# Another order of the steps of a two-part kernel: x transposes and halo copies earlier in SyncE's queue, head and tail sums of a chunk side by side

## The chip, the cores and the metric

The kernel runs on one core of a Trainium2 chip. The metric is the device time of one execution in microseconds (us), the median over runs. The engines are named as the profile names them: PE (TensorE matmuls; PEld its weight loads), DVE (VectorE), ACT (ScalarE), POOL (GpSimd) and SP (SyncE, which here only issues DMAs). A "q" behind an engine (SPq, POOLq) means its queue of instructions.

## The reference

Two independent layers are computed on inputs of 2048 positions x 448 channels, and their outputs stand side by side in one array of 2048 x 896 (bfloat16).

```python
# part A: a linear state space layer with complex, diagonal state
Lam_bar = exp(dt * Lam);  B_bar = ((Lam_bar - 1) / Lam)[:, None] * Bmat
Bu = einsum("bld,pd->blp", x, B_bar)
h[t] = Lam_bar * h[t-1] + Bu[t]                       # t = 0 .. 2047
y = 2 * einsum("blp,dp->bld", h, Cmat).real + x * Dskip
# part B: attention of 16 heads (28 wide) to 8 positions: t, t-2, ..., t-14
q, k, v = split(x @ wqkv)
logits[t, w] = q[t] . k[t - 2w] * 28 ** -0.5          # -1e9 where t - 2w < 0
o[t] = sum_w softmax(logits[t])[w] * v[t - 2w]
out = o @ wo
```

## The kernel before

Each part is cut into small methods, and one string, `ORDER` (L751), lists the calls: `plan` (L786) reads it word by word and calls the method, so the string sets the order of the instructions on PE, DVE, ACT and SP. Each of these engines executes its own instructions in that order and waits only for semaphores; so a step that waits holds everything behind it on its engine. POOL's order is left to a scheduler. A step's name is a letter and its arguments; a trailing A or V says whether ACT or DVE carries out a copy from PSUM. PSUM tiles come from three rings: "mm" (four buffers), "pt" (two) and "lg" (two). A PE step takes a buffer when one has been released by its copy, so a late copy can hold PE.

Part B works on four chunks c of 512 positions.

- `P.c.g.w`: projection of q (w = 0) or k (w = 1), group g of 128 channels, four matmuls (L191); g = 3 is the tail, the last 64 channels of q and k together. `p...` copies it out (L83 on ACT, L88 on DVE). Trailing arguments pick some of the four slices of the contraction.
- `R.c.s` (DVE, L239): products of q with four shifted windows of k; `T.c` (L244): the same for the tail. `S.c.s` (PE, L254) and `St.c.s` (L261) sum them over each head with 32-column matmuls, s = 0, 1 being windows 0-3 and 4-7: the head sums and the tail sums. `St.0.1` adds the mask (L266).
- `s`, `mt`, `mr`, `mb`, `ms`, `me`: copy of the logits (L83), transposes (L276), max (DVE, L280), its copy (L83 or L88), its subtraction on PE (L290), exp (ACT, L296). `N`, `n`: back-transposes with sums (L305), reciprocal and product (DVE, L311, L312).
- `V.j`, `v.j`: v for positions 16p + j (L216, and a copy). `Z` (SP, L183) and `H` (L228, L229) are DMAs that write the halo, the 14 positions ahead of each partition's 16: `H.r0.r1` needs the v that it copies, `H.0.6` v.2 to v.7, `H.6.10` v.8 to v.11, `H.10.14` v.12 to v.15.
- `u.j.w` (DVE, L325): attention times v for positions j to j+3 and window w; `d` (DVE, L330) adds one of these to the sum; `f` (POOL, L334) adds one to another by an accumulating DMA. `tu.j` (SP, L338) transposes the result by DMA, and for the last four `tm`, `te` do it on PE, ACT and DVE (L347, L351, L352). `O`, `o`, `od`: the product with wo (L358), copy, output DMA (L373; L368 for the last two).

Part A has a state of 448 complex numbers, seven tiles m of 128. The 16 positions of a partition are handled as four a times four b.

- `X.a.b` (SP, L418 and L419): two DMA transposes that load x for positions 4a + b. `L.b.m` (PE, L600) multiplies them by the input matrix; it needs X.0.b to X.3.b. For odd b it adds the state of b - 1 (L603), for b = 3 also that of 1 (L605).
- `pp`, `pe`, `tb` (four pieces), `pg`, `M`, `B`, `b`: parameters, tables of sines and exponents, the matrices (L558 on DVE, 14 instructions L563 on ACT), the input matrix (L571, copy, and a memset on POOL, L577).
- `la`, `le`, `ro`, `sn`, `bk`, `be`: the last positions, and a scan over the partitions' blocks in two parts (0 and 1) that goes PE, DVE, PE, DVE, PE, ACT. `G`, `g`, `C`, `c`: corrections of the states. With V, one addition on DVE (L674, L693); with A, an identity matmul more on PE (L665, L683) and a copy on ACT (L676, L695).
- `sc` (SP, L582): four DMA transposes of the output matrix. `Y.a.b`, `y.a.b`: output (11 matmuls, L708, L711), copy to one of three buffers `ya`, output DMA on SP (L717).

SP issues, ahead of all steps, the loads of part B's x (L106, L108), weights and B matrices; then its DMAs stand in the order of the string.

Of the kernel before, what the change touches and what calls it, by code (L numbers as in the profile page):

```python
# [748 lines left out]


ORDER = """  # L751
    xa X.2.1 P.0.1.1.0.3 pp X.3.1 lw X.2.2 X.0.1 X.0.0 P.0.0.1.0.3 P.0.1.0.0.3 P.0.1.0.3.4 p.0.1.0.A P.0.2.1
    P.0.1.1.3.4 p.0.1.1.A P.0.0.1.3.4 p.0.0.1.A X.1.2 p.0.2.1.A P.0.0.0.0.3 P.0.0.0.3.4 P.0.2.0 p.0.0.0.A
    P.1.0.1 p.0.2.0.A pe tb R.0.1.1.2 P.1.2.0 p.1.2.0.A P.1.1.1 P.2.1.1 R.0.0.1.2 p.1.0.1.A p.2.1.1.A X.3.2
    P.0.3.0 p.0.3.0.A R.0.0.0.1 P.1.2.1 p.1.1.1.A p.1.2.1.A P.2.0.1 R.0.0.2.3 P.1.1.0 p.1.1.0.A P.1.0.0 S.0.0
    R.0.1.2.3 P.1.3.0 T.0 St.0.0 R.0.1.0.1 S.0.1 p.1.0.0.A p.2.0.1.A R.1.0 V.14 Z P.3.1.1 p.1.3.0.A tb p.3.1.1.A
    tb tb P.2.2.0 P.2.0.0 v.14.A R.1.1 X.3.0 P.2.1.0 p.2.1.0.A St.0.1 p.2.2.0.A P.3.0.1 p.3.0.1.A V.7 M.3.V
    v.7.A P.2.3.0 P.2.2.1 X.0.3 s.0.A T.1 mt.0 p.2.3.0.A P.3.2.1 p.3.2.1.A S.1.0 St.1.0 mr.0 p.2.2.1.A V.13 V.15
    S.1.1 St.1.1 p.2.0.0.A V.9 v.15.A P.3.2.0 pg B.3 mb.0.V R.2.0 ms.0 v.13.A v.9.A p.3.2.0.A V.2 me.0 V.8 v.8.A
    T.2 V.4 R.2.1 s.1.A B.0 b.3.A P.3.0.0 p.3.0.0.A P.3.1.0 p.3.1.0.A mt.1 mr.1 X.1.1 b.0.A S.2.0 P.3.3.0 mb.1.V  # L760
    p.3.3.0.A St.2.0 S.2.1 St.2.1 s.2.A V.1 v.1.A v.2.A v.4.A R.3.0 V.3 B.2 V.10 B.5 v.10.A ms.1 V.6 V.0 me.1
    V.11 T.3 v.3.A R.3.1 b.2.A mt.2 v.11.V mr.2 S.3.0 V.12 St.3.0 v.6.A b.5.A X.2.0 M.1.A S.3.1 St.3.1 B.1 X.0.2
    s.3.A L.2.0 mb.2.V pa M.4.V X.1.0 mt.3 H.6.10 V.5 ms.2 M.2.V mr.3 mb.3.V v.5.V L.2.2 v.12.A al l.2.0.A me.2
    ms.3 M.0.V sk H.10.14 L.0.0 b.1.A me.3 N.0 l.2.2.V N.3 n.3 n.0 L.0.3 u.0.3 u.0.4 lc v.0.A H.0.6 L.0.1
    l.0.1.A u.0.2 u.0.0 B.4 l.0.0.A L.1.1 L.2.3 f.0.2 u.0.5 B.6 l.0.3.A L.1.0 l.1.0.A u.0.1 u.0.6 f.0.4 u.0.7
    L.0.2 l.0.2.A N.12 d.0.1 N.6 L.2.1 l.1.1.A L.1.2 L.0.5 X.2.3 L.1.3 l.2.3.A n.12 n.6 d.0.2 u.4.3 l.2.1.A
    u.4.1 X.3.3 X.1.3 b.4.A l.1.3.A L.3.1 L.3.3 l.3.1.A L.0.4 d.0.4 l.0.5.A l.1.2.A L.3.2 l.3.2.A f.0.6 L.2.4
    N.15 b.6.A n.15 d.0.6 l.3.3.A L.3.0 l.0.4.A L.1.4 l.3.0.A L.2.5 L.0.6 N.9 sa la.0 l.2.5.A l.1.4.A L.1.5
    l.1.5.A L.3.5 l.3.5.A u.4.0 u.4.5 u.4.4 f.4.4 le.0 l.0.6.A tu.0 l.2.4.A sm u.4.2 f.4.2 ro.0 sn.0 L.2.6
    l.2.6.A L.3.4 l.3.4.A O.2.1 bk.0 be.0.A d.4.1 L.1.6 l.1.6.A L.3.6 l.3.6.A G.2.V G.0.V n.9 G.1.A u.4.6 la.1  # L770
    g.1.A G.3.V u.4.7 C.1.1.A O.0.0 g.2.V C.1.2.A u.8.1 le.1 c.1.2.A o.0.0.A ro.1 g.3.V c.1.1.A sc C.1.3.A
    C.0.2.A c.0.2.A g.0.V c.1.3.A f.4.6 C.2.2.A c.2.2.A sn.1 O.0.1 bk.1 be.1.A Y.3.3 G.6.V y.3.3.A u.8.5 o.0.1.A
    d.4.2 C.1.0.V u.8.7 C.0.0.A G.4.A g.4.A c.0.0.A O.2.0 C.0.3.V g.6.V G.5.A g.5.A u.8.3 Y.1.3 y.1.3.A C.0.6.A
    c.0.6.A c.0.3.V C.1.5.A c.1.5.A c.1.0.V u.8.0 d.4.4 d.4.6 tu.4 C.1.4.V c.1.4.V Y.0.3 u.8.4 C.0.5.V c.0.5.V
    y.0.3.A u.8.2 Y.2.3 y.2.3.A C.0.4.V d.8.1 c.0.4.V o.2.0.A C.1.6.A c.1.6.A Y.1.1 C.0.1.V c.0.1.V Y.2.1
    C.2.5.V u.8.6 c.2.5.V od.0 C.2.4.V o.2.1.A od.2 c.2.4.V Y.1.0 C.2.6.V u.12.0 y.1.1.A y.2.1.A Y.3.1 c.2.6.V
    u.12.1 Y.2.0 f.8.2 d.8.2 O.4.0 O.4.1 y.1.0.A f.8.4 o.4.0.A o.4.1.A od.4 d.8.4 Y.0.0 u.12.4 f.8.6 C.2.0.V
    d.8.6 tu.8 c.2.0.V u.12.3 u.12.2 f.12.2 Y.3.0 O.6.0 y.3.1.A u.12.5 f.12.4 y.0.0.A C.2.1.V c.2.1.V C.2.3.V
    y.3.0.A O.6.1 Y.0.1 c.2.3.V Y.2.2 Y.3.2 O.8.0 O.8.1 u.12.6 d.12.1 d.12.6 Y.0.2 y.0.1.A O.10.1 o.6.0.A
    o.6.1.A o.8.0.A od.6 u.12.7 d.12.7 y.3.2.A o.8.1.A y.2.0.A od.8 d.12.2 d.12.4.0.2 O.10.0 d.12.4.2.4 tm.12  # L780
    Y.1.2 o.10.0.A o.10.1.A od.10 y.1.2.V tm.14 y.0.2.A te.12 O.12.0 O.12.1 te.14 O.14.0 O.14.1 o.12.0.A
    o.12.1.A od.12 y.2.2.A o.14.0.S o.14.1.S
"""


# [52 lines left out]
```

## Time and profile before

| what | value |
|---|---|
| time, median of 13 runs | 145.25 us (144.59 to 147.35) |
| the profiled execution: its time, its span | 144.59 us, 142.9 us |
| granted clock of PE in the profiled execution | 1.00 |
| busy: ACT, POOL | 82.2 us (58%), 55.0 us (39%) |
| halo copies issued on SP | 53.66 to 58.53 us |
| last three X issued on SP | 58.57 to 69.01 us |
| first scan on DVE (`sn.0`), second (`sn.1`) | 85.00 to 87.68, 94.89 to 96.98 us |
| start of the last PE transposes (`tm.12`, `tm.14`) | 133.54, 135.46 us |

The span is that of one execution on the chip, from its first to its last instruction; times within it count from its start. In a timeline row stand the start, the time taken, the engine, the line and operation, what is written and read, the shape, the number of instructions, and in brackets the engine's idle time before it and what ended that. Matmuls overlap: one of 512 columns is shown with 379 ns, and the next can start after 216 ns.

### The profile page before, as it was taken

The page shows a single profiled execution, that of the slowest core. Times are in us where ns is not written, and L with a number is a line of the kernel's source. Part 1 is how long each engine was busy: PE and PEld are TensorE (multiplying, and loading weights), DVE is VectorE, ACT ScalarE, POOL GpSimd, SP SyncE. Part 2 cuts the span into 40 slices and gives each one's busy share as a digit, 9 for nine tenths or more (in the row PEclk, how much of TensorE's full clock was granted, in tenths as well). Part 3 has the DMA queues.
Part 4 walks back from the last instruction along what each step waited for, and adds up shares of the span by engine and source line. Part 5 has one row for each costly group of instructions (what it writes and reads, how often), then busy time and mean ns, then how long its engine had stood idle before and what let it go on. Part 6 is the DMA issues. An engine that isn't in the chain of part 4 may idle for free.

```text
span 142.9 us, 2560 instructions
## 1 busy us (share of the span) xinstructions
PE 134.3 (94%) x920; PEld 71.0 (50%) x920; DVE 124.1 (87%) x167; ACT 82.2 (58%) x178; POOL 55.0 (39%) x108
## 2 busy tenths in 40 slices
...
GB/s 104 288 193 202 169 232 71 70 68 87 98 127 133 142 109 175 260 90 138 212 81 0 137 184 202 92 128 0 32 40 223 218 260 165 160 223 225 109 152 135
DMA packets 36426, 20.49 MB, mean 143 GB/s; under 512 B 27762, under 2 KB 34048, under 8 KB 36413
## 3 DMA queue, kind: packets, MB, share of 16 engines
...
## 4 chain that ended last, share of the span: by engine, by line
PE 46%; DVE 25%; DMA 13%; SPq 6%; ACT 4%; issue 4%; ACTq 0%
DVE pr L239 10%; PE u_ps L600 9%; PE y_ps L711 9%; PE qk_ps L191 9%; DMA out_dram<-ya 9%; PE wo_ps L358 6%; DMA xaT<-in_A_x_dram 4%; SPq L418 3%; DVE prt L244 2%; PE warm L68 2%; DVE mat L558 2%; SPq L419 2%; DVE mx L280 2%; PE u_ps L603 2%; PE y_ps L708 1%
## 5 line engine op out<-in xcount | busy, mean ns | idle before, releaser
L600 PE MATMUL u_ps<-xaT,Bcat 128*128 128x512 bf16 x112 | 27.7, 379 | 2.5 <-DMA xaT<-in_A_x_dram 2.5
L325 DVE TENSOR_TENSOR pvt<-attn,vd 128x1792 bf16<-128x1792 bf16 x28 | 29.5, 1084 | 0.1
L334 POOL DMA_DIRECT2D pvt<-pvt x11 | 9.5, 865 | 51.5 <-DVE pvt L325 51.3
L239 DVE TENSOR_TENSOR pr<-qT,kT 128x2048 bf16<-128x2048 bf16 (+1 forms) x12 | 27.4, 2314 | 0.0
L83 ACT CAST u<-u_ps 128x512 bf16<-128x512 f32 x27 | 14.7, 593 | 16.7 <-PE u_ps L605 6.8
L711 PE MATMUL y_ps<-C,u 128*128 128x448 bf16 x112 | 23.8, 353 | 0.0
L191 PE MATMUL qk_ps<-xbT,wqkv_nat 128*128 128x512 bf16 x96 | 22.5, 379 | 0.1
L330 DVE TENSOR_TENSOR pvb<-pvb,pvt 128x1792 bf16<-128x1792 bf16 (+1 forms) x18 | 18.6, 1036 | 1.4 <-DMA pvt<-pvt 1.3
L600 PEld LDWEIGHTS <-Bcat 128*128 128x128 bf16 x112 | 10.5, 98 | 13.9 <-DMA xaT<-in_A_x_dram 3.0
L83 ACT CAST ya<-y_ps 128x448 bf16<-128x448 f32 x15 | 7.9, 536 | 13.9 <-PE y_ps L711 8.7
L191 PEld LDWEIGHTS <-wqkv_nat 128*128 128x128 bf16 x96 | 9.1, 98 | 10.9 <-issue 1.1
L216 PE MATMUL v_ps<-wqkv_nat,xbT 128*128 128x448 bf16 x64 | 14.1, 358 | 0.0
L358 PE MATMUL wo_ps<-wo_p,oT 128*128 128x448 bf16 x64 | 13.8, 352 | 0.0
L711 PEld LDWEIGHTS <-u 128*128 128x128 bf16 x112 | 9.9, 98 | 7.3
L83 ACT CAST qT<-qk_ps 128x512 bf16<-128x512 f32 (+1 forms) x20 | 9.7, 496 | 4.9 <-PE qk_ps L191 4.7
L83 ACT CAST yb<-wo_ps 128x448 bf16<-128x448 f32 x14 | 7.3, 539 | 7.6 <-PE wo_ps L358 7.6
L83 ACT CAST kT<-qk_ps 128x512 bf16<-128x512 f32 (+3 forms) x23 | 10.1, 459 | 1.3 <-PE qk_ps L191 1.0
L216 PEld LDWEIGHTS <-xbT 128*128 128x128 bf16 x64 | 8.5, 147 | 3.6 <-issue 1.3
L358 PEld LDWEIGHTS <-oT 128*128 128x128 bf16 x64 | 6.2, 98 | 5.8 <-issue 0.2
L179 POOL TENSOR_SCALAR_AFFINE_SELECT IS<-IS 128x16 bf16<-128x16 bf16 x8 | 8.8, 1098 | 0.1
L83 ACT CAST vd<-v_ps 128x448 bf16<-128x448 f32 x14 | 7.2, 536 | 2.3 <-PE v_ps L216 2.3
L693 DVE TENSOR_TENSOR u<-co,u 128x512 bf16<-128x512 f32 x12 | 7.9, 684 | 0.0
(178 smaller groups left out, 208.4 us busy)
## 6 DMA issues: line engine op xcount, KB each, us to landing
...
xaT<-in_A_x_dram SPq DMA_TRANSPOSE x32, 4.4
```

Of the source, the lines that this page charges most:

```text
L83: nc.scalar.copy(out, in_)
L179: G.affine_select(out=self.IS[:, NCH:], in_=self.IS[:, NCH:], compare_op=ALU.not_equal, fill=1.0, base=-H * w, pattern=[[-1, H]], channel_ ...
L191: self.nc.tensor.matmul(self.ps_t[c, g, which][:], lhsT=wv[:, k], rhs=self.xT[:, k, c * CH:(c + 1) * CH], start=(k == 0), stop=(k == KT - 1))
L216: self.nc.tensor.matmul(ps[:], lhsT=xv[:, k, j, :], rhs=self.wn[:, k, 2, :], start=(k == 0), stop=(k == KT - 1))
L239: self.nc.vector.tensor_tensor(pr[:, :, g0:g1, :], self.qT[:, c, g0:g1].unsqueeze(1).to_broadcast([NCH, 4, n, CH]), self.windows(self.kT[: ...
L325: self.nc.vector.tensor_tensor(self.pv_buf(j0, w), self.at[:, w, j0:j0 + 4, :].unsqueeze(2).to_broadcast([NCH, 4, DH, H]), self.vd[:, off: ...
L330: self.nc.vector.tensor_tensor(acc, acc, self.pv_buf(j0, w)[:, i0:i1], op=ALU.add)
L334: self.nc.gpsimd.dma_start(a_, b_, accum_op=ALU.add)
L358: self.nc.tensor.matmul(ps[:], lhsT=oT[:, s + k, :], rhs=self.wo_p[:, KT * n + k, :], start=(k == 0), stop=(k == KT - 1))
L600: nc.tensor.matmul(ps4[:], lhsT=self.Bcat[:, k, m, :], rhs=self.xT[:, b, k], start=(k == 0), stop=(b % 2 == 0 and k == KT - 1))
L693: self.nc.vector.tensor_tensor(h_, ps, h_, op=ALU.add)
L711: nc.tensor.matmul(ps[:], lhsT=self.state(m, a, b), rhs=self.C[:, m, :], start=False, stop=(m == NM - 1), skip_group_check=True)
```

## The change

Only the string is changed. 478 steps stand in another order, and 23 copies, additions and matrices go to the other engine (with A, a G or C has its identity matmul). For the sums, chunk 0 changes from `S.0.0 ... St.0.0 ... S.0.1 ... St.0.1`, with projections and V between, to four sums with no other PE step between; chunks 1 to 3 likewise, and in chunk 1 from two pairs to one row of four.

| on SP, in order | before | after |
|---|---|---|
| ahead of the first H | Z and X 2.1, 3.1, 2.2, 0.1, 0.0, 1.2, 3.2, 3.0, 0.3, 1.1, 2.0, 0.2, 1.0 | Z and X 3.2, 0.0, 0.1, 1.1, 3.1, 3.0, 2.0, 1.0, 1.3, 2.2, 2.1, 1.2 |
| then | H.6.10, H.10.14, H.0.6, X 2.3, 3.3, 1.3 | H.10.14, X.2.3, H.6.10, X.0.2, H.0.6, X 3.3, 0.3 |
| then | tu.0, sc | sc, tu.0 |

To the other engine go: from ACT to DVE `p.3.0.1`, `v.2`, `M.1`, `g.4`, `g.5`, `c.0.2`, `c.0.6`, `c.1.1`, `c.1.2`, `c.1.5`, `c.1.6`; from DVE to ACT `v.5`, `v.11`, `mb.1`, `l.2.2`, `g.0`, `g.2`, `g.3`, `c.0.1`, `c.0.4`, `c.1.4`, `c.2.3`, `y.1.2`.

The diff, cut to the places that the prediction speaks of:

```diff
-    P.0.3.0 p.0.3.0.A R.0.0.0.1 P.1.2.1 p.1.1.1.A p.1.2.1.A P.2.0.1 R.0.0.2.3 P.1.1.0 p.1.1.0.A P.1.0.0 S.0.0
-    R.0.1.2.3 P.1.3.0 T.0 St.0.0 R.0.1.0.1 S.0.1 p.1.0.0.A p.2.0.1.A R.1.0 V.14 Z P.3.1.1 p.1.3.0.A tb p.3.1.1.A
-    tb tb P.2.2.0 P.2.0.0 v.14.A R.1.1 X.3.0 P.2.1.0 p.2.1.0.A St.0.1 p.2.2.0.A P.3.0.1 p.3.0.1.A V.7 M.3.V
...
-    s.3.A L.2.0 mb.2.V pa M.4.V X.1.0 mt.3 H.6.10 V.5 ms.2 M.2.V mr.3 mb.3.V v.5.V L.2.2 v.12.A al l.2.0.A me.2
-    ms.3 M.0.V sk H.10.14 L.0.0 b.1.A me.3 N.0 l.2.2.V N.3 n.3 n.0 L.0.3 u.0.3 u.0.4 lc v.0.A H.0.6 L.0.1
...
-    L.0.2 l.0.2.A N.12 d.0.1 N.6 L.2.1 l.1.1.A L.1.2 L.0.5 X.2.3 L.1.3 l.2.3.A n.12 n.6 d.0.2 u.4.3 l.2.1.A
-    u.4.1 X.3.3 X.1.3 b.4.A l.1.3.A L.3.1 L.3.3 l.3.1.A L.0.4 d.0.4 l.0.5.A l.1.2.A L.3.2 l.3.2.A f.0.6 L.2.4
...
+    P.1.1.1 p.1.1.1.A P.2.2.0 p.2.2.0.A P.2.1.1 p.2.1.1.A pe tb X.0.1 P.1.2.0 R.0.0.1.2 R.0.1.1.2 P.1.1.0
+    p.1.1.0.A P.2.1.0 P.1.0.0 p.2.1.0.A tb tb p.1.2.0.A R.0.1.2.3 P.1.0.1 p.1.0.1.A P.1.3.0 p.1.3.0.A R.0.0.2.3
+    R.0.0.0.1 S.0.0 T.0 St.0.0 R.0.1.0.1 S.0.1 St.0.1 s.0.A V.14 P.3.1.1 p.3.1.1.A p.1.0.0.A P.3.2.0 Z tb pg
+    mt.0 mr.0 T.1 p.3.2.0.A sk mb.0.V P.1.2.1 p.1.2.1.A R.1.0 V.8 v.8.A X.1.1 P.2.0.1 P.2.2.1 p.2.0.1.A
...
+    X.1.0 me.0 B.6 R.1.1 S.1.0 St.1.0 b.6.A S.1.1 b.0.A St.1.1 P.3.0.0 p.3.0.0.A p.3.0.1.V B.3 V.13 X.1.3 b.3.A
+    P.3.2.1 v.14.A s.1.A lc V.3 R.2.0 V.11 mt.1 p.3.2.1.A T.2 v.11.A R.2.1 B.1 mr.1 mb.1.A V.10 v.10.A S.2.0
+    St.2.0 S.2.1 St.2.1 v.13.A s.2.A v.3.A X.2.2 V.15 P.3.3.0 R.3.0 p.3.3.0.A mt.2 V.5 V.0 R.3.1 v.15.A X.2.1
+    V.2 ms.1 T.3 V.12 V.6 B.2 b.1.A v.0.A S.3.0 St.3.0 S.3.1 pa me.1 v.2.V v.12.A v.5.A St.3.1 s.3.A mr.2 mb.2.V
...
+    B.4 M.3.V L.0.1 al me.3 l.0.0.A l.0.1.A N.0 n.0 L.0.3 l.0.3.A b.4.A X.2.3 v.7.A H.6.10 N.3 n.3 u.0.0 v.4.A
+    B.5 L.1.1 l.1.1.A u.0.1 L.1.0 l.1.0.A N.15 n.15 b.5.A L.0.2 u.0.3 l.0.2.A X.0.2 L.1.3 L.2.6 l.2.6.A L.2.4
+    u.0.2 L.2.2 l.2.4.A d.0.1 N.12 u.0.4 H.0.6 L.0.5 n.12 l.0.5.A L.2.1 l.2.1.A u.0.5 u.0.7 N.9 n.9 L.2.0 L.0.6
+    l.1.3.A l.0.6.A l.2.0.A X.3.3 N.6 n.6 L.0.4 u.4.0 l.2.2.A l.0.4.A X.0.3 L.2.3 L.1.2 l.1.2.A L.3.2 f.0.2
...
+    u.8.6 u.8.3 C.2.0.V C.0.0.A c.2.0.V u.8.7 Y.2.3 C.1.4.A Y.0.3 o.2.1.A od.2 f.8.6 u.8.2 od.0 c.0.0.A f.8.2
+    c.1.4.A y.1.3.A C.2.4.V C.1.5.V y.2.3.A u.8.5 c.2.4.V c.1.5.V O.6.0 C.0.3.V c.0.3.V f.8.4 C.0.5.V O.6.1
...
+    d.8.2 c.1.6.V C.2.6.V d.8.4 c.2.6.V u.12.2 Y.3.2 Y.2.2 d.8.6 u.12.4 Y.1.1 tu.8 Y.1.0 Y.0.1 y.2.2.A Y.1.2
...
```

More of the change, by code (lines that the diff above doesn't have):

```diff
@@ L751 @@
 ORDER = """
-    xa X.2.1 P.0.1.1.0.3 pp X.3.1 lw X.2.2 X.0.1 X.0.0 P.0.0.1.0.3 P.0.1.0.0.3 P.0.1.0.3.4 p.0.1.0.A P.0.2.1
-    P.0.1.1.3.4 p.0.1.1.A P.0.0.1.3.4 p.0.0.1.A X.1.2 p.0.2.1.A P.0.0.0.0.3 P.0.0.0.3.4 P.0.2.0 p.0.0.0.A
-    P.1.0.1 p.0.2.0.A pe tb R.0.1.1.2 P.1.2.0 p.1.2.0.A P.1.1.1 P.2.1.1 R.0.0.1.2 p.1.0.1.A p.2.1.1.A X.3.2
-    P.0.3.0 p.0.3.0.A R.0.0.0.1 P.1.2.1 p.1.1.1.A p.1.2.1.A P.2.0.1 R.0.0.2.3 P.1.1.0 p.1.1.0.A P.1.0.0 S.0.0
-    R.0.1.2.3 P.1.3.0 T.0 St.0.0 R.0.1.0.1 S.0.1 p.1.0.0.A p.2.0.1.A R.1.0 V.14 Z P.3.1.1 p.1.3.0.A tb p.3.1.1.A
@@ L757 @@
-    tb tb P.2.2.0 P.2.0.0 v.14.A R.1.1 X.3.0 P.2.1.0 p.2.1.0.A St.0.1 p.2.2.0.A P.3.0.1 p.3.0.1.A V.7 M.3.V
[L758 to L761, printed above, removed]
@@ L762 @@
-    V.11 T.3 v.3.A R.3.1 b.2.A mt.2 v.11.V mr.2 S.3.0 V.12 St.3.0 v.6.A b.5.A X.2.0 M.1.A S.3.1 St.3.1 B.1 X.0.2
-    s.3.A L.2.0 mb.2.V pa M.4.V X.1.0 mt.3 H.6.10 V.5 ms.2 M.2.V mr.3 mb.3.V v.5.V L.2.2 v.12.A al l.2.0.A me.2
-    ms.3 M.0.V sk H.10.14 L.0.0 b.1.A me.3 N.0 l.2.2.V N.3 n.3 n.0 L.0.3 u.0.3 u.0.4 lc v.0.A H.0.6 L.0.1
-    l.0.1.A u.0.2 u.0.0 B.4 l.0.0.A L.1.1 L.2.3 f.0.2 u.0.5 B.6 l.0.3.A L.1.0 l.1.0.A u.0.1 u.0.6 f.0.4 u.0.7
-    L.0.2 l.0.2.A N.12 d.0.1 N.6 L.2.1 l.1.1.A L.1.2 L.0.5 X.2.3 L.1.3 l.2.3.A n.12 n.6 d.0.2 u.4.3 l.2.1.A
@@ L767 @@
-    u.4.1 X.3.3 X.1.3 b.4.A l.1.3.A L.3.1 L.3.3 l.3.1.A L.0.4 d.0.4 l.0.5.A l.1.2.A L.3.2 l.3.2.A f.0.6 L.2.4
[L768 to L781, printed above, removed]
```

17 lines of the change are left out of this document (16 added, 1 removed).

## The prediction, made before the changed kernel was run

> **What bounds the kernel now.** I read the page's busy line first, then TensorE's (PE's) timeline for its gaps, then SyncE's queue for what ended the largest gap, then the other engines' timelines for distances.
>
> ```profile
> PE 134.3 (94%) x920; PEld 71.0 (50%) x920; DVE 124.1 (87%) x167; ACT 82.2 (58%) x178; POOL 55.0 (39%) x108
> ```
>
> PE and VectorE (DVE) are both nearly full. So a new order gains only what PE and DVE stand idle now, or what PE loses between matmuls. PE's timeline shows two long gaps after the start:
>
> ```profile
> 68.28 0.38 PE L603 MATMUL u_ps<-u,mat 128*128 128x512 bf16 x1
> 71.12 1.04 PE L600 MATMUL u_ps<-xaT,Bcat 128*128 128x512 bf16 x4 [2.46 <-DMA xaT<-in_A_x_dram]
> ...
> 119.65 0.38 PE L685 MATMUL co<-u,mat 128*128 128x512 bf16 x1
> 120.94 0.36 PE L708 MATMUL y_ps<-Dg,xaT 128*128 128x128 bf16 x4 [0.92 <-ACT ya L83]
> ```
>
> Start to start, the first costs 2.84 - 0.22 = 2.6 us, the second 1.29 - 0.22 = 1.1. The first ends with a transpose of part A's x that stood last in SyncE's queue, behind three halo copies (L228, L229) that wait for ScalarE and DVE:
>
> ```profile
> 56.96 0.70 SPq L228 DMA_DIRECT2D vd<-vd  x1
> 57.70 0.82 SPq L229 DMA_DIRECT2D vd<-vd  x1
> 58.57 2.00 SPq L418 DMA_TRANSPOSE xaT<-in_A_x_dram  x1
> 60.62 1.23 SPq L419 DMA_TRANSPOSE xaT<-in_A_x_dram  x1
> ...
> 65.18 2.01 SPq L418 DMA_TRANSPOSE xaT<-in_A_x_dram  x1
> 67.24 1.77 SPq L419 DMA_TRANSPOSE xaT<-in_A_x_dram  x1
> ```
>
> The last pair is issued at 65.2, and the chain of waits has 5.9 us from there to 71.1. A third loss is in no gap. Full matmuls and the 32-column sums follow each other at a price:
>
> ```profile
> 30.50 1.03 PE L191 MATMUL qk_ps<-xbT,wqkv_nat 128*128 128x512 bf16 x4
> 31.46 0.83 PE L254 MATMUL lg<-pr,ones 128*32 128x512 bf16 x12
> 32.12 0.39 PE L261 MATMUL lg<-prt,ones 128*32 128x256 bf16 x8
> 32.44 1.73 PE L216 MATMUL v_ps<-wqkv_nat,xbT 128*128 128x448 bf16 x8
> ...
> 43.49 0.40 PE L261 MATMUL lg<-prt,ones 128*32 128x256 bf16 x8
> 43.72 0.82 PE L254 MATMUL lg<-pr,ones 128*32 128x512 bf16 x12
> ```
>
> Four full matmuls take 4 x 0.216 = 0.86 (0.87 from 29.42 to 30.28 elsewhere), but 0.96 here before the sums: 0.10 to enter. Eight tail sums take 0.23 when sums follow (43.49 to 43.72) and 0.32 when a full matmul follows: 0.09 to leave. A group costs 0.19.
>
> **The change, part by part.** All times are us of the profiled execution. I put the row's durations, start to start, in the new order, engine by engine, and made a step wait where its producer is later.
>
> *Groups of sums.* S and St form nine groups now; in the new order each chunk's four stand together: four groups. 5 x 0.19 = -0.95 on PE. The Trainium skill ("TensorEngine Tiling (Array Packing)", Key Properties) says that a switch of mode drains TensorE. A whole drain would be what a matmul outlasts its issue, 379 - 216 = 163 ns, 1.6 for ten switches; the rows show 0.10 and 0.09, and I go by the rows.
>
> *Evictions changed hands.* Corrections through ScalarE, with an identity matmul on PE, go from 9 to 7 (-2 x 0.216), groups G from 3 to 4 (+0.16): PE -0.27. DVE gains M.1 (1.0), two corrections (1.2), p.3.0.1 (0.6), v.2 (0.5) and loses v.11, v.5 (1.2), l.2.2 (0.6), a max copy (0.3), one G (0.5), and y.1.2 at the end: +0.7 before its last addition. ScalarE loses M.1 (3.5); it is 58% busy, so that is not the path.
>
> *To 22 us.* The fourth slice of K arrives as now (8.08). Then 19 + 36 matmuls at 0.216 bring PE to 19.9, where chunk 0's sums start. ScalarE carries a table load group (1.75) and three sines (2.0) between the evictions now; the tightest, p.1.1.0, ends at 17.8 and its buffer is wanted at 18.2. DVE's seven products are the same and end at 20.3, wanted at 20.9. No wait; the four sums end at 21.9, now 22.1 with one set of St missing.
>
> *22 to 55: sums against products.* In DVE's queue the tables (2.7) and the g matrix (2.9) now stand ahead of chunk 1's products, which ran at 20.3 and 26.5. From 20.3: 2.7 + 2.9 + max 0.6 + T.1 1.1 + 0.3 = 27.9, R.1.0 to 31.1, R.1.1 to 34.4; then p.3.0.1 0.6, R.2.0 to 38.2, T.2 to 39.4, R.2.1 to 42.6, max 0.6, R.3.0 and R.3.1 to 49.8, T.3 to 50.9 (3.27 a product, 1.14 a T). PE comes to S.1.1 at 33.9, S.2.1 at 41.7, St.3.0 at 50.5: waits of 0.5, 0.9 and 0.4, where the trace has none. The max copies of chunks 2 and 3 (52.4, 55.2) cost 0.3, a buffer 0.15. Waits 2.2 against 0.95 saved. mb.1 is now on ScalarE and waits for DVE's max from 40.2 to 43.2; queued behind it are v.10, v.13, s.2, v.3 and p.3.3.0, whose buffers PE needs from 44.4: the 0.15 is theirs. PE starts L.0.0 at 55.5; now 56.9 with two L more done (1.7), so 55.2. Up to here the change is 0.3 behind.
>
> *55 to 98: the transposes.* GpSimd's queue is as now up to its memsets of Bcat, which all come ahead of the first accumulate: nothing. SyncE issues 12 of 16 x tiles and the zero row ahead of the first halo copy: 16.9 + 12 x 2.75 (the mean of 13 to 53.5) + 1.0 = 50.8. Then H.10.14, X.2.3, H.6.10, X.0.2 to 60: landed by 62 to 63, wanted by L.2.6 at 63. H.0.6 waits for v.4, whose eviction is queued behind b.4 and v.7: 60.6. So X.3.3 and X.0.3 leave at 62.2 and 65.4 (3.2 each as at 58.6), hardly earlier than now, and land at 65.4 + 5.9 = 71.3. What helps is PE's order: the L of b = 3 that need them stand behind nearly all others, at 72.4. The 2.6 goes, with 1.1 to spare. The four transposes of C (6.8) now stand ahead of tu.0 in SyncE's queue, from 69 to 76; tu.0 can start at 83. The skill ("DMA: Bandwidth & Descriptors", Issuing engines are not separate DMA queues) speaks against a gain from the place in one queue: SyncE's and GpSimd's transfers share 16 engines. By it X.0.3 would land late beside accumulates; the 5.9 was measured beside such, so the sum holds either way.
>
> H.0.6 lands about 66.2 (4.1 after issue as now), wanted by u.0.5 at 67.6. DVE starts n.0 at 58.2, has no gap to le.0, waits 0.2, and ends the first scan at 85.6 (now 87.6) with 1.0 more done. PE is at bk.0 at 85.6 (now 87.7 with 0.3 more left). The second scan ends at 93.7 (now 96.9); Y.3.3 ends at 97.5 (now 98.7) with one O (0.76) and 0.98 of G less to come.
>
> *98 to the end.* PE's rest is G 0.33, 20 matmuls of corrections 4.31, 15 Y 22.8, 12 O 9.1, transposes 0.8: 37.3, so 134.9 without waits, where it is 139.1. DVE's rest from 93.7 is 16 products 16.1, ten additions 10.3, halves 1.2, G 1.4, 12 corrections 7.2: 36.2, to 129.9. The 1.1 ahead of a Y (a copy to ya that waits for an output) I take as gone: the first copy that waits, y.0.3 at 104.4, wants y.3.3 landed, which leaves at 100.4. What is late next is the accumulating DMAs (L334):
>
> ```profile
> 116.55 2.22 DVE L330 TENSOR_TENSOR pvb<-pvb,pvt 128x1792 bf16<-128x1792 bf16 x2 [0.56 <-DMA pvt<-pvt]
> ...
> 132.86 1.16 DVE L330 TENSOR_TENSOR pvb<-pvb,pvt 128x896 bf16<-128x896 bf16 x2 [0.43 <-DMA pvt<-pvt]
> ```
>
> Now the three of j = 8 are issued at 107.7, 109.3, 112.5 and land at 114.1, 116.5, 120.1. In the new order they follow u.8.7, u.8.2, u.8.5: 103.8, 104.8, 105.8, closer. From the first issue to the last landing the three of j = 0 took 9.6 and these 12.4; the ends are 4.2 (one alone, at 91.9) and 3 x 7.6 = 22.8. I take 11.7, near to the same three now: 115.5. d.8.4 stands at 113.9 in DVE's queue; it waits 1.6, and behind it c.2.6 (117.2), which Y.3.2 on PE wants at 115.8 (PE 1.5), and d.8.6, which SyncE's tu.8 and five output DMAs behind it wait for. DVE's last halves then start at 130.6 to 131.2 (now 132.9), tm.12 at 131.3 (now 133.5), and from there the tail is the same: 9.4 to the span's end. 140.7, and 0.2 for the small gaps that 1% of PE's rows show between 55 and 85: span 140.9.
>
> The profiled execution took 144.59 for 142.9, 1.7 around the span: 142.6. It is the shortest of 13, whose median is 145.25, 0.66 higher; so I forecast **143.2**.
>
> **Rivals.** *No new waits at the end*: the accumulates land by 114, PE's 134.9 holds; 142.9 - 4.2 = 138.7, with 0.66 + 1.7: 141.0. For: the one at 91.9 landed in 4.2. Against: four outputs Y leave together with them. *It does not do what it says*: the last four x tiles stay behind halo copies, and H.0.6 waits for v.4. If the pair takes 3.8 each (the slowest row), or ScalarE's queue behind mb.1 costs what the 2.6 gains, the result is 145.2 to 145.8. For: 1.1 to spare is small. *Slower*: the accumulates of j = 8 hold DVE. Every us that f.8.4 lands after 115.5 moves c.2.6, d.8.6, tu.8 and the end; from 118.3 on (14.5 after the first issue) the time is over 146, 0.5% above the median. If each takes 7.6 in a row, 126.5, 11 later: 154; if they follow at the 4.1 at which f.12.4 followed f.12.2 after a first of 7.6, 119.6: 147.3. For: the three start within 2 us, with tu.4 and outputs. Against: now they followed at 2.4 and 3.6.
>
> **How the numbers follow.** Forecast 0.46 (own range 142.0 to 144.5); no new waits 0.17 (141.0); no gain 0.14 (145.5); slower 0.23 (147.3, up to 154). 0.5% is about what a measurement here can tell. Faster 0.63, same 0.14, slower 0.23. The range reaches from the second case to the nearer price of the slow one: 140.6 to 147.3.
>
> **What would show it.** Right: no wait on xaT on PE; four groups of sums; DVE products of chunk 1 after the tables; PE idle some 0.5, 0.9, 0.4 us ahead of S.1.1, S.2.1, St.3.0; DVE waiting for pvt around 114 to 116. Wrong: a wait on xaT ahead of L.2.6 or L.3.2; PE idle behind ScalarE's copies between 43 and 50; waits on ya or pvt over 3 us after 98.

## The result and the profile after

The changed kernel takes **143.23 us** (median of 11 runs, 142.46 to 143.89); the kernel before, run beside it, 145.55 (48 runs). The ratio is 0.9866, with a 95% interval of 0.9841 to 0.989: faster by 1.3%, and the forecast was 143.2. The profiled execution has a span of 140.9 (forecast 140.9) and took 142.59. Ratios leave out the slower executions, in which the chip granted TensorE a lower clock (mostly 0.975 to 0.988 in the kernel before); without them the kernel before comes to some 145.2 (143.23 / 0.9866).

The busy line of the page after:

```profile
PE 133.2 (95%) x919; PEld 71.7 (51%) x919; DVE 124.5 (88%) x166; ACT 80.3 (57%) x166; POOL 59.2 (42%) x108
```

PE is busy 1.1 us less, DVE 0.4 more. The gap ahead of the L of b = 3 is gone. In PE's timeline after, the place at which `L.1.2` ends and `L.3.2` begins (start, time, engine, line; a wait would stand in brackets):

```profile
72.78 0.38 PE L603 MATMUL u_ps<-u,mat 128*128 128x512 bf16 x1
73.00 1.03 PE L600 MATMUL u_ps<-xaT,Bcat 128*128 128x512 bf16 x4
```

73.00 follows 72.78 by the 0.22 of a matmul. SyncE's queue after, from the last halo copy to the last two pairs of x transposes, now X.3.3 and X.0.3 (before, X.3.3 and X.1.3):

```profile
61.17 0.55 SPq L228 DMA_DIRECT2D vd<-vd  x1
...
62.65 2.06 SPq L418 DMA_TRANSPOSE xaT<-in_A_x_dram  x1
...
66.03 1.25 SPq L418 DMA_TRANSPOSE xaT<-in_A_x_dram  x1
```

The last pair is issued at 66.0, against 65.2 before: not earlier at all. The sums of chunk 2 stand in one group, and wait inside it:

```profile
41.28 0.83 PE L254 MATMUL lg<-pr,ones 128*32 128x512 bf16 x12
41.94 0.39 PE L261 MATMUL lg<-prt,ones 128*32 128x256 bf16 x8
42.95 0.83 PE L254 MATMUL lg<-pr,ones 128*32 128x512 bf16 x12 [0.61 <-DVE pr L239]
43.59 0.41 PE L261 MATMUL lg<-prt,ones 128*32 128x256 bf16 x8
```

The most telling view is one that the prediction did not use: what VectorE waited for from 9 us to the end of its last addition (at 134.0 before, 132.05 after). The columns are the operation that waited, its releaser, us in total, times, the longest. Before:

```profile
DVE rec L311 <- PE tp L305: 1.4, 1, 1.4
DVE pvb L330 <- DMA pvt<-pvt: 1.3, 3, 0.6
DVE rt L638 <- PE g3A L632: 0.6, 1, 0.6
DVE gsc L651 <- PE rotA L645: 0.5, 1, 0.5
DVE cosE L504 <- ACT shE L499: 0.2, 1, 0.2
```

After:

```profile
DVE pvb L330 <- DMA pvt<-pvt: 1.0, 2, 0.9
```

In the changed kernel this view has no wait of VectorE between 9 and 113 us; what is left of its idle time there are gaps too short to be listed. Adding up its own rows gives an account of the whole execution: when its first real operation starts (L449, when the parameters have arrived), its work, its idle time up to the end of the last addition, and what follows that. The four sum to the span by construction. What they show is where a saving can come from.

| profiled execution | start | work | idle | after the last addition | span |
|---|---|---|---|---|---|
| before | 6.88 | 121.78 | 5.36 | 8.86 | 142.9 |
| after | 6.84 | 122.73 | 2.47 | 8.83 | 140.9 |

2.9 less idle time, 0.95 more work: 2.0 in all, as the spans have it. Of the idle time, the waits listed above are 4.0 before and 1.0 after. A few tenths of such an account say nothing: executions with the same VectorE instructions have 121.39 to 122.36 us of work (before, experiments 1, 2, 7 and 8) and 122.30 to 122.95 (after, experiments 3, 4 and 9).

### The profile page after: what moved, and what is told of

It reads as the page before. It is cut to its first block, busy times and chain, and to the rows that moved or that the text cites. A ratio compares the mean times of both kernels' runs of the same rounds, so it can differ in the third digit from the quotient of the medians.

```text
span 140.9 us, 2554 instructions
## 1 busy us (share of the span) xinstructions
PE 133.2 (95%) x919; PEld 71.7 (51%) x919; DVE 124.5 (88%) x166; ACT 80.3 (57%) x166; POOL 59.2 (42%) x108
## 5 line engine op out<-in xcount | busy, mean ns | idle before, releaser
L83 ACT CAST u<-u_ps 128x512 bf16<-128x512 f32 x28 | 16.0, 591 | 12.8 <-PE u_ps L600 6.0
L600 PEld LDWEIGHTS <-Bcat 128*128 128x128 bf16 x112 | 10.6, 98 | 11.2
L179 POOL TENSOR_SCALAR_AFFINE_SELECT IS<-IS 128x16 bf16<-128x16 bf16 x8 | 12.9, 1619 | 0.1
L693 DVE TENSOR_TENSOR u<-co,u 128x512 bf16<-128x512 f32 x14 | 9.1, 685 | 0.0
L83 ACT CAST vd<-v_ps 128x448 bf16<-128x448 f32 x15 | 7.7, 542 | 1.6 <-PE v_ps L216 1.6
```

Source lines behind the costliest of these rows:

```text
L83: nc.scalar.copy(out, in_)
L179: G.affine_select(out=self.IS[:, NCH:], in_=self.IS[:, NCH:], compare_op=ALU.not_equal, fill=1.0, base=-H * w, pattern=[[-1, H]], channel_ ...
L600: nc.tensor.matmul(ps4[:], lhsT=self.Bcat[:, k, m, :], rhs=self.xT[:, b, k], start=(k == 0), stop=(b % 2 == 0 and k == KT - 1))
L693: self.nc.vector.tensor_tensor(h_, ps, h_, op=ALU.add)
```

## Experiments

Times are medians of each kernel's runs; a ratio is to the kernel before on the same chip, with its 95% interval. Experiments 1 to 4 ran side by side, then 5 to 8, then 9 to 11, then 12. Ratios are best compared inside such a group; across groups, and with the changed kernel's 0.9866, which stands by itself, a difference of 0.3% tells nothing.

### Experiment 1: of the change, only TensorE's order of the L

```diff
-    b.4.A l.1.3.A L.3.1 L.3.3 l.3.1.A L.0.4 d.0.4 l.0.5.A l.1.2.A L.3.2 l.3.2.A f.0.6 L.2.4
-    N.15 b.6.A n.15 d.0.6 l.3.3.A L.3.0 l.0.4.A L.1.4 l.3.0.A L.2.5
+    b.4.A l.1.3.A L.0.4 L.2.4 d.0.4 l.0.5.A l.1.2.A l.0.4.A f.0.6
+    N.15 b.6.A n.15 d.0.6 L.1.4 L.3.1 L.3.3 l.3.1.A L.3.2 l.3.3.A L.3.0 l.3.2.A l.3.0.A L.2.5
```

> The kernel before, and only TensorE's order of part A's local states changed: L.0.4, L.2.4, N.15 and L.1.4 go ahead of the four L of b = 3 (L.3.1, L.3.3, L.3.2, L.3.0); SyncE's order and the sums stay. Theory (the gain of the change is the 2.6 us stall on the last x transposes, and TensorE's order of the L takes it away): the three L are 4 + 4 + 5 matmuls x 0.216 = 2.8 us of work, so the wait of 2.46 on xaT goes; VectorE's waits of 1.43, 0.60 and 0.52 up to the first scan go with it, the scan ends some 2.4 earlier; span 142.9 - 2.4 = 140.5, ratio 0.983. Rival 1 (the transposes' place in SyncE's queue does it): the wait on xaT shrinks by what stands ahead and the time hardly moves, because the second scan or the end is bound elsewhere: ratio 0.995 to 1.0. Rival 2 (nine groups of sums against four is the gain): ratio 1.0, as nothing of the sums is changed.

Measured: 142.92 us, ratio **0.9843** (0.9807 to 0.988). That is the whole gain of the change, from a few steps out of 478. VectorE's waits in the same stretch as above:

```profile
DVE pvb L330 <- DMA pvt<-pvt: 1.2, 3, 0.7
DVE gsc L651 <- PE rotA L645: 0.5, 1, 0.5
DVE cosE L504 <- ACT shE L499: 0.2, 1, 0.2
```

The 1.4 ahead of L311 and the 0.6 ahead of L638 are gone. Both were TensorE's stall, handed on: `N.15` and `la.0` stood behind the L that waited. The 0.5 inside the first scan (L651) stays, so it was no part of the stall. VectorE's idle time falls from 5.36 to 3.27. Its last addition ends at 132.08, within 0.03 of the changed kernel. Both rivals fall.

### Experiment 2: only SyncE's order, carried further

```diff
-    pa M.4.V X.1.0 mt.3 H.6.10
+    pa M.4.V X.1.0 mt.3 X.2.3 X.3.3 X.1.3 H.6.10
...
-    L.1.2 L.0.5 X.2.3 L.1.3
+    L.1.2 L.0.5 L.1.3
...
-    u.4.1 X.3.3 X.1.3 b.4.A
+    u.4.1 b.4.A
```

> The kernel before, and only SyncE's order changed: X.2.3, X.3.3 and X.1.3 go ahead of the three halo copies (H.6.10, H.10.14, H.0.6). Theory: the wait on xaT on TensorE goes, since the last pair is issued some 60 us after the start instead of 65.2, but the halo copies are issued some 9 us later (three pairs of 3.2 each), H.0.6 lands at 70 to 71, and VectorE, which had no slack ahead of u.0.3 to u.0.7, waits 4 to 7 us for vd; span 142.9 + 2 to 5 = 145 to 148, ratio 1.01 to 1.035. Rival 1 (the place in SyncE's queue is what gains): the wait on xaT goes and VectorE finds other work: span 140.5, ratio 0.983.

Measured: 149.51 us, ratio 1.0317 (1.0268 to 1.0366). The wait on xaT is gone, and VectorE has this one:

```profile
DVE pvt L325 <- DMA vd<-vd: 6.4, 1, 6.4
```

The place in SyncE's queue does decide when the transposes land; but three pairs ahead of the halo copies are paid by VectorE, and dearly. Rival 1 falls. Fewer pairs ahead of them were not tried in the kernel before.

### Experiment 9: have the last transposes become earlier?

The changed kernel with `L.3.1` at an early turn again; SyncE's own order stays as it is in the changed kernel.

```diff
-    L.2.0 L.0.6 l.1.3.A l.0.6.A l.2.0.A X.3.3
+    X.3.3 X.0.3 L.2.0 L.3.1 l.1.3.A l.2.0.A
...
-    L.0.4 u.4.0 l.2.2.A l.0.4.A X.0.3 L.2.3
+    L.0.4 L.0.6 u.4.0 l.2.2.A l.3.1.A l.0.4.A l.0.6.A L.2.3
...
-    sa d.0.2 L.3.1 l.3.3.A
+    sa d.0.2 l.3.3.A
```

> The changed kernel, and one L of b = 3 (L.3.1) put back ahead of N.6, L.0.4, L.0.6, L.2.3 and L.1.2 on TensorE, where its turn comes at 69.1; SyncE's and VectorE's order stay. Theory (the last transposes land near 71.3, as late as before, and only TensorE's order takes the wait away): a wait on xaT of 2.0 to 2.3 comes back, N.6 is 2.2 + 1.3 later, VectorE idles some 2 ahead of n.6, and all behind it is 2 later: span 142.5 to 143, ratio to before 0.997 to 1.003. Rival (the place in SyncE's queue makes them land early): no wait on xaT, ratio 0.985 to 0.988.

Measured: 143.99 us, ratio 0.9968 (0.9942 to 0.9993): three quarters of the gain are lost. In PE's timeline the wait is back:

```profile
68.30 1.03 PE L600 MATMUL u_ps<-xaT,Bcat 128*128 128x512 bf16 x4
70.75 1.04 PE L600 MATMUL u_ps<-xaT,Bcat 128*128 128x512 bf16 x4 [1.42 <-DMA xaT<-in_A_x_dram]
```

The transposes have landed by 70.75; before, by 71.12. The wait is 1.4 and not 2.0 to 2.3, as they came 0.6 before the 71.3 that I had from the prediction. The first scan starts 1.6 later than in the changed kernel (85.17, 83.55), `tm.12` only 1.07 later (132.64, 131.57): VectorE now comes so late that the accumulates make it wait 0.6 instead of 1.0.

### Experiment 8: of the change, the L and the groups of sums

Experiment 1, with nine groups made four; the order of VectorE's products is untouched.

```diff
-    S.0.0 R.0.1.2.3 P.1.3.0 T.0 St.0.0 R.0.1.0.1 S.0.1 p.1.0.0.A
+    P.1.3.0 S.0.0 R.0.1.2.3 T.0 St.0.0 R.0.1.0.1 S.0.1 St.0.1 p.1.0.0.A
...
-    p.2.1.0.A St.0.1 p.2.2.0.A
+    p.2.1.0.A p.2.2.0.A
...
-    S.1.0 St.1.0 mr.0 p.2.2.1.A V.13 V.15 S.1.1 St.1.1
+    mr.0 V.13 p.2.2.1.A V.15 S.1.0 St.1.0 S.1.1 St.1.1
...
-    S.2.0 P.3.3.0 mb.1.V p.3.3.0.A St.2.0 S.2.1 St.2.1
+    P.3.3.0 mb.1.V p.3.3.0.A S.2.0 St.2.0 S.2.1 St.2.1
...
-    S.3.0 V.12 St.3.0 v.6.A b.5.A X.2.0 M.1.A S.3.1 St.3.1
+    V.12 S.3.0 St.3.0 v.6.A b.5.A X.2.0 M.1.A S.3.1 St.3.1
```

> The kernel of the first experiment (before, with the L of b = 3 later), and the nine groups of sums made four: P.1.3.0 ahead of S.0.0 and St.0.1 behind S.0.1, V.13 and V.15 ahead of S.1.0, P.3.3.0 ahead of S.2.0, V.12 ahead of S.3.0; SyncE's order and VectorE's are unchanged. All products are ready by then, so TensorE's row shortens by 5 x 0.19 = 0.95. Theory A (VectorE sets the time): the 0.95 turns into waits on VectorE, the time is that of the first experiment: ratio to before 0.982 to 0.986. Theory B (TensorE sets it): 0.95 less than the first experiment: ratio 0.977.

Measured: 142.44 us, ratio 0.9817 (0.9768 to 0.9866), 0.0026 or 0.4 us under experiment 1 and inside its interval. TensorE's waits from 19 to 58 us, where experiment 1 has none:

```profile
PE lg L254 <- DVE pr L239: 0.4, 2, 0.2
```

I had expected all products to be ready; two were not, because TensorE now came earlier. It starts the last chunk's max subtraction (`ms.3`) at 56.07 and not 56.74, and 0.37 of that was there ahead of the first sum: of the 0.95, 0.3 is left at 56 us. Theory A gave nothing, theory B 0.95; by the trace, the measurement is close to A, and it cannot tell 0 from 0.4. The ratio alone would not rule out B, whose 0.977 lies at the edge of its interval.

### Experiment 4: the groups split again

The changed kernel, its four groups made eight by steps that fill its waits.

```diff
-    S.0.1 St.0.1 s.0.A V.14 P.3.1.1
+    S.0.1 V.14 St.0.1 s.0.A P.3.1.1
...
-    S.1.0 St.1.0 b.6.A S.1.1 b.0.A St.1.1 P.3.0.0 p.3.0.0.A
+    S.1.0 St.1.0 b.6.A P.3.0.0 S.1.1 b.0.A St.1.1 p.3.0.0.A
...
-    St.2.0 S.2.1 St.2.1 v.13.A s.2.A v.3.A X.2.2 V.15 P.3.3.0
+    St.2.0 V.15 S.2.1 St.2.1 v.13.A s.2.A v.3.A X.2.2 P.3.3.0
...
-    V.6 B.2 b.1.A v.0.A S.3.0 St.3.0 S.3.1
+    V.6 b.1.A v.0.A S.3.0 B.2 St.3.0 S.3.1
```

> The changed kernel, and the four groups of sums split into eight: V.14 goes ahead of St.0.1, P.3.0.0 ahead of S.1.1, V.15 ahead of S.2.1, B.2 ahead of St.3.0. Theory (a group costs 0.19 on TensorE, and the long groups wait for VectorE's products): 4 x 0.19 = 0.76 more of switches, against waits of 0.6 at S.2.1 and 0.2 of the 0.4 at St.3.0 that the steps between now fill; L.0.0 starts the same within 0.3 us and the time is the same within 0.3%. Rival 1 (the number of groups is the gain): span 140.9 + 0.8 = 141.7, ratio to the changed kernel 1.006. Rival 2 (switches cost nothing, the waits do): span 140.1, ratio 0.994.

Measured: 142.69 us, ratio 0.9826 (0.9784 to 0.9867): not slower than the changed kernel. From the first sum to `ms.3` it takes 35.53 us, the changed kernel 35.83. The 0.76 of switches was paid with time in which TensorE would have waited for products. Rival 1 falls. Rival 2's 0.8 is not in the profile, which has 0.30; the ratio does not decide, as it lies between "the same" and rival 2 (0.996 of the changed kernel's, where 1.0 and 0.994 were expected).

### Experiment 7: the wait on ya, taken out of the kernel before

```diff
-        self.lgb = self.pool.tile([NCH, CH], bf16, name="lgb", tag="lgb", bufs=2)
+        self.lgb = self.pool.tile([NCH, CH], bf16, name="lgb", tag="lgb", bufs=1)
...
-        ya = self.pool.tile([NCH, D], bf16, name="ya", tag="ya", bufs=3)
+        ya = self.pool.tile([NCH, D], bf16, name="ya", tag="ya", bufs=4)
```

> The kernel before, and a fourth buffer for part A's output copies (ya); the room for it comes from the copies of the logits, which get one buffer instead of two. It takes away the 1.1 that TensorE waits ahead of the Y at 120.9. Theory A (VectorE sets the time; no step of VectorE follows from these Y before its last halves): TensorE waits as much later, ahead of tm.12, and the time is the same: ratio 0.998 to 1.002. Theory B (the prediction's sum, in which this 1.1 is gained): ratio 0.992.

Measured: 145.15 us, ratio 1.0023 (0.9989 to 1.0057). TensorE's waits from 19 to 134 us:

```profile
PE u_ps L600 <- DMA xaT<-in_A_x_dram: 2.2, 2, 2.1
PE u_ps L605 <- issue: 0.2, 1, 0.2
PE y_ps L708 <- DVE u L693: 0.2, 1, 0.2
```

The 0.9 on ya (1.1 start to start) is gone and the time is the same. Theory B's 0.992 lies outside the interval: that wait was worth nothing that can be measured. Nothing in this profile waits for the one buffer that the copies of the logits have left, so the room taken from them is not what ate a gain. What theory A expects in its place, `tm.12` waiting for VectorE's last halves, is there with 0.16 only:

```profile
135.43 0.56 PE L347 MATMUL pt_o<-ident,pvb 128*128 128x128 bf16 x7 [0.16 <-DVE pvb L330]
```

But the profile is of an execution of 146.60 us, in which PE is busy 1.6 longer than in that of before. Where the 1.1 went is therefore not shown.

### Experiment 3: the wait for the accumulates, filled

```diff
-    d.8.2 c.1.6.V C.2.6.V d.8.4 c.2.6.V u.12.2 Y.3.2 Y.2.2 d.8.6
+    d.8.2 c.1.6.V C.2.6.V c.2.6.V u.12.2 d.8.4 Y.3.2 Y.2.2 d.8.6
```

> The changed kernel, and only VectorE's order at the accumulating DMA's wait: c.2.6 and u.12.2 go ahead of d.8.4. Theory (the wait for pvt holds c.2.6 and through it TensorE at Y.3.2): VectorE's wait of 0.88 is filled by c.2.6 (0.6) and a part of u.12.2 (1.0), TensorE's wait of 0.9 at Y.3.2 goes, and nothing takes its place: span 140.9 - 0.7 to 0.9 = 140.0 to 140.2, ratio to the changed kernel 0.994. Rival (VectorE is the bound of the end, as d.8.6 and the last halves come later by c.2.6 and u.12.2): the wait moves to tm.12, span 140.7 to 141.2, ratio 1.0.

Measured: 142.61 us, ratio 0.9827 (0.9794 to 0.986), 0.996 of the changed kernel's: between the theory's 0.994 and the rival's 1.0, with overlapping intervals, so the time does not decide. TensorE no longer waits at `Y.3.2`, and waits here:

```profile
131.43 0.56 PE L347 MATMUL pt_o<-ident,pvb 128*128 128x128 bf16 x7 [1.07 <-DVE pvb L330]
```

`tm.12` starts 0.14 earlier than in the changed kernel (131.57), or 0.55 if both are counted from VectorE's start (7.25 and 6.84). Of this, VectorE's idle time is 0.12 (2.35 and 2.47) and its work 0.43, which is within the scatter of the same work. So the wait of 0.88 was not gained: `c.2.6` now waits 0.52 for its own matmul (L685). The trace speaks for the rival: a wait of TensorE is exchanged for another, since the last halves on VectorE come when they come.

### Experiments 5 and 6: VectorE's work, less and more

Experiment 5 gives the changed kernel's `p.3.0.1.V` and `v.2.V` back to ScalarE; experiment 6 gives `l.0.5.A` and `l.0.6.A` to VectorE. No step moves.

> The changed kernel, and two copies from PSUM, p.3.0.1 (0.69 on VectorE) and v.2 (0.61), given back to ScalarE; no step moves. Theory A (VectorE's queue, which has no gap from 8.9 to 112.9 us in the changed kernel, sets the time): 1.3 less work there, so its last addition ends near 130.8 instead of 132.05 and the time falls by 0.9 to 1.3: span 139.6 to 140.0, ratio to before 0.978. Theory B (TensorE's own work sets the time, as the prediction summed it): TensorE's 0.6 and 0.4 of waits ahead of S.2.1 and St.3.0 shrink and the time falls by those 1.0 too, but without that share the first scan would not come earlier; in B the gain ends where TensorE waits for nothing, at 0.6 to 1.0. Theory C (ScalarE's copies come late and take the place): ScalarE is 0.6 later at 36 to 40 and at 49 to 50, where it then idles 0.7 and 2.3; nothing gained if TensorE waits for buffers there: ratio 0.985.

> The changed kernel, and two copies of part A's states (l.0.5, l.0.6) moved from ScalarE to VectorE, some 0.6 to 0.7 each, between 67 and 72 us. Theory A (VectorE sets the time): 1.2 to 1.4 later from there to the end: span 142.1 to 142.3, ratio to before 0.994 to 0.996. Theory B (TensorE sets it): TensorE loses at most what a buffer comes late, 0 to 0.4, and VectorE catches up in its waits of 0.9 at d.8.4: ratio 0.985 to 0.988.

Measured: experiment 5 takes **141.99 us**, ratio **0.9792** (0.9736 to 0.9848), the fastest kernel of this study, 0.7% under the changed kernel. Experiment 6 takes 143.93, ratio 0.9912 (0.987 to 0.9955). VectorE's account of 5 has 1.34 less work than the changed kernel's. Its profile was taken of the longest of its six executions, though (143.14, start 7.57, idle 3.63); there the idle time has eaten the work saved, so where the gain of the others lies is not seen. In 6 it can be: work +1.08, idle -0.37, last addition 0.75 later, for 0.0046 x 145.5 = 0.7 us in the ratio. All that VectorE waits for in 6 is

```profile
DVE pvb L330 <- DMA pvt<-pvt: 0.7, 1, 0.7
```

Between the two, side by side, lie 2.42 us of VectorE's work and 0.0120 x 145 = 1.7 us of time: copies on VectorE have a price. Which theory is right the times do not settle. 5 fits theory A (0.978) and theory B (0.6 to 1.0 less than the changed kernel, 0.980 to 0.982); 6 lies half-way between A (0.994 to 0.996) and B (0.985 to 0.988). The trace of 6 speaks for A, with a price 0.4 to 0.7 too large as the wait for the accumulates gave way: but for this wait of 0.7 VectorE has none. TensorE waits 0.5 there for a copy that VectorE now makes, which B also allowed for (0 to 0.4).

### Experiments 10 to 12: more copies off VectorE, and what that needs

On top of experiment 8, `v.11`, `v.5` and `l.2.2` go to ScalarE, and `L.2.5` ahead of the L of b = 3, `n.0` ahead of `n.3`:

```diff
-    mt.2 v.11.V mr.2
+    mt.2 v.11.A mr.2
...
-    ms.2 M.2.V mr.3 mb.3.V v.5.V L.2.2 v.12.A al l.2.0.A me.2
+    ms.2 M.2.V mr.3 mb.3.V L.2.2 v.5.A v.12.A al l.2.0.A me.2
...
-    N.0 l.2.2.V N.3 n.3 n.0 L.0.3
+    N.0 l.2.2.A N.3 n.0 n.3 L.0.3
...
-    L.1.4 L.3.1 L.3.3 l.3.1.A L.3.2 l.3.3.A L.3.0 l.3.2.A l.3.0.A L.2.5 L.0.6 N.9 sa la.0 l.2.5.A l.1.4.A
+    L.1.4 L.2.5 L.3.1 L.3.3 l.3.1.A L.3.2 l.3.3.A L.3.0 l.3.2.A l.3.0.A L.0.6 N.9 sa la.0 l.2.5.A l.1.4.A
```

> The kernel of the eighth experiment (before, L of b = 3 later, four groups of sums), and three copies moved from VectorE to ScalarE: v.11, v.5 (0.6 each) and l.2.2 (0.7); L.2.5 goes ahead of the L of b = 3, n.0 ahead of n.3. Theory (time = VectorE's start + its work + its idle time + 8.9): work 1.9 less, of which n.0 gives back 0.4 to 1.1, as it then waits for TensorE's N.0 some 57.4 after the start: 0.8 to 1.5 less than the eighth, ratio to before 0.972 to 0.977. Rival (TensorE is the bound as soon as VectorE is relieved): no less than the eighth, 0.982.

Measured: 147.27 us, ratio 1.0198 (1.0157 to 1.0239), a clear miss. PE's timeline says why, at three of the L of b = 3:

```profile
76.54 1.02 PE L600 MATMUL u_ps<-xaT,Bcat 128*128 128x512 bf16 x4 [0.67 <-ACT u L83]
...
78.67 1.02 PE L600 MATMUL u_ps<-xaT,Bcat 128*128 128x512 bf16 x4 [0.67 <-ACT u L83]
```

Each waits for the copy of the L just ahead, so one buffer of the four was left to them. `L.1.4` and `L.2.5` hold two, because their copies stand behind those of the L of b = 3 in ScalarE's queue, and `L.2.4` holds the third, as its copy comes later still. (In experiment 8 `L.2.4` and `L.1.4` hold two; with the other two nothing waits.) VectorE gets the sum:

```profile
DVE rt L638 <- PE g3A L632: 3.7, 1, 3.7
```

Experiment 11 moves two corrections (`C.1.4`, `C.0.5`) to ScalarE as well.

> The kernel of the tenth experiment, and two corrections (C.1.4 and C.0.5) moved from VectorE to ScalarE, each with an identity matmul more on TensorE (0.216). Theory (VectorE sets the time): 2 x 0.68 = 1.4 less work, of which the wait for the accumulating DMAs of j = 8 gives back what they land too late, 0.4 to 0.9: another 0.5 to 1.0 less, ratio to before 0.966 to 0.973. Rival (TensorE is the bound by then): 0.43 more than the tenth.

Measured: 149.62 us (147.56 to 152.04), ratio 1.0298 (1.0231 to 1.0364), slower again by 1.4 where the rival had 0.43, though the two intervals just touch. In the trace a correction's matmul (L685) waits 2.1 for a buffer that a ya copy is late to release, and VectorE waits 2.3 and 1.1 for corrections' matmuls. Experiment 12 is the tenth with the copies in the order in which buffers are needed:

```diff
-    mb.3.V L.2.2 v.5.A v.12.A al l.2.0.A me.2
+    mb.3.V L.2.2 v.12.A al l.2.0.A me.2 v.5.A
...
-    L.1.4 L.2.5 L.3.1 L.3.3 l.3.1.A
+    L.1.4 L.2.5 L.3.1 L.3.3 l.1.4.A l.2.5.A l.3.1.A
...
-    sa la.0 l.2.5.A l.1.4.A L.1.5
+    sa la.0 L.1.5
```

> The kernel of the tenth experiment, and the copies in ScalarE's queue put in the order in which TensorE needs the buffers: v.12 ahead of v.5, l.1.4 and l.2.5 ahead of l.3.1. Theory (the tenth was slow because L.1.4 and L.2.5 held two of the four mm buffers while the L of b = 3 ran, so each waited 0.84 for the copy of the one before, and v.5 held L.2.2): these waits and VectorE's 3.7 ahead of le.0 go; what is left of the 1.9 of copies is what n.0 starts earlier than in the eighth, 0.4, since TensorE's N.0 comes no earlier: ratio to before 0.977 to 0.982. Rival (the three copies themselves are too much for ScalarE): no less than the tenth, 1.015 to 1.02.

Measured: 143.07 us, ratio 0.9898 (0.9862 to 0.9934). TensorE's four waits of 0.67 and VectorE's 3.7 are gone, so the buffers were the cause of the tenth's loss. But of the copies nothing is gained: VectorE has 1.1 less work than in experiment 8 and waits at two places where it did not wait there,

```profile
DVE rec L311 <- PE tp L305: 1.2, 1, 1.2
DVE mx L280 <- PE pt_m L276: 0.7, 1, 0.7
```

both at 54 to 59 us, where TensorE and ScalarE set the pace. The expected 0.4 did not come; the theory had N.0 no later than in experiment 8, and it came 1.0 later (58.41 against 57.38), as TensorE waits 0.9 for a copy of the logits ahead of `mt.3`.

## Why the prediction was right, and where it was not

The cause was right, and was one of several that the sum counted. **The stall of 2.6** went by TensorE's order of the L and not by SyncE's queue, as the prediction's 55 to 98 had it: the pair leaves at 66.0 (forecast 65.4); in experiment 9, where it leaves at the same time, it has landed by 70.75 (71.3); `L.3.2` starts at 73.0 (72.4). Experiments 1, 2 and 9 show it from three sides.

**What the savings were worth** I read on the wrong engine. The prediction lists PE's savings (0.95, 0.27, 2.6, 1.1) as if each could count. Experiment 7 measures the 1.1 of ya at nothing, experiment 8 the 0.95 of the groups at 0 to 0.4. The stall counted because VectorE waited behind it twice (1.4 and 0.6), and both waits go in experiment 1: 2.0 of the 2.6. That the number came out all the same has a reason: in the end stage the prediction summed VectorE's rest too and let its last halves set `tm.12`. It had 131.3; the trace has 131.57,

```profile
131.57 0.56 PE L347 MATMUL pt_o<-ident,pvb 128*128 128x128 bf16 x7
```

and 9.3 from there to the end (forecast 9.4). The last step of the forecast was luck: it took over 0.66 from the profiled execution to the median, and it was 0.64 again, though nothing says that a profiled execution must be among the shortest. A few of the prediction's sums are 0.1 off (50.8 for 50.9, 134.9 for 134.8, 126.5 for 126.6); nothing hangs on that.

**Groups of sums.** Four, as forecast. A switch costs what was read: in experiment 4 a full matmul follows the last tail sum after 0.20, where another sum follows after 0.10; and a sum follows a V matmul after 0.28, another V matmul after 0.19. The Trainium skill ("TensorEngine Tiling (Array Packing)", Key Properties) has TensorE drain at a switch; the 163 ns that I worked out for a whole drain are not seen in either direction.

**Evictions changed hands.** VectorE's work grew by 0.95, of which a few tenths are scatter; the forecast was 0.7. Experiments 5 and 6 show that copies on VectorE have a price.

**22 to 55.** Chunk 1's products start at 28.00 (27.9). The waits on products came at S.2.1 (0.61, forecast 0.9) and St.3.0 (0.19, forecast 0.4), on the max copy 0.32 (0.3); the 0.15 for a buffer did not come. The wait of 0.5 at S.1.1 did not come, because one that I had missed stood ahead of it: `V.14`, the first V, starts at 22.53 after a wait of 0.57. In the changed kernel and in experiment 3:

```profile
22.53 0.95 PE L216 MATMUL v_ps<-wqkv_nat,xbT 128*128 128x448 bf16 x4 [0.57 <-ACT kT L83]
22.62 0.95 PE L216 MATMUL v_ps<-wqkv_nat,xbT 128*128 128x448 bf16 x4 [0.39 <-DMA wqkv_nat<-in_B_wqkv_dram]
```

The first profile puts that down to a copy; but the copy that `V.14` needs (`p.1.2.0`) has ended at 20.6, and in experiments 3, 5 and 6 the same wait (to 22.62, 22.75 and 22.95) is put down to the load of v's weights. So those arrive some 22.5 us after the start in the changed kernel. The trace of before has `V.14` at 22.12 without a wait, so there they had arrived by then; why they come later now is not shown. The prediction took ScalarE's buffers into account here and not the input loads. `L.0.0` is at 56.0, forecast 55.5.

**98 to the end.** The 0.5 stayed up to here and grew: `Y.3.3` ends at 98.3 (97.5). The three accumulates leave at 104.4, 105.4 and 106.4 (103.8 to 105.8), and `d.8.4` starts at 115.64, 11.2 after the first (forecast 11.7), with a wait of 0.88 (1.6):

```profile
115.64 1.09 DVE L330 TENSOR_TENSOR pvb<-pvb,pvt 128x1792 bf16<-128x1792 bf16 x1 [0.88 <-DMA pvt<-pvt]
```

So VectorE's lateness was taken from its wait. Two errors of half a microsecond cancelled there, through this wait; in experiments 6 and 9 it gives way in the same manner.

**The rivals.** "No new waits at the end" (141.0) was priced on TensorE alone. Experiment 3 takes the wait out of TensorE's row at `Y.3.2` and gets 1.07 at `tm.12` in its place; its 142.61 us are far from 141.0. The slow case needed f.8.4 to land 14.5 after the first issue; it took 11.2.

Not settled: what the 12 x tiles ahead of the halo copies are worth in the changed kernel, as no kernel here undoes that alone; where the 1.1 of ya went in experiment 7; and where experiment 5 gains, as said.
